# Weight and z preparation cut into stages a step apart, in an attention and GLU kernel

## Chip, core, metric

One of the eight cores of a Trainium2 chip runs the whole kernel. The metric is the device time of one execution in microseconds; lower is better. The time before is 2075.76 us, the median of three runs (2073.78 to 2076.12).

## What is computed

```python
scores = z @ z.T / S                      # per batch; B, S = 4, 3008; d_qk = 64
attn = np.maximum(scores, 0) ** 2
x = u * (attn @ v)                        # d_model = 256
x = x.reshape(B * S, 256)
gate = 1 / (1 + np.exp(-(x @ w_gate)))    # weights 256 x 1536, float64 in memory
out = (gate * (x @ w_val)) @ w_out        # 1536 x 256; out 12032 x 256, float32
```

The inputs u, v and z are float32. The three weights come as float64, and the kernel turns each into two 32-bit parts itself.

## The kernel before

To keep float32 accuracy every factor is split in a high part, which TensorE multiplies exactly, and a low part, the rest. A product takes three matmuls: high by high, high by low, low by high. Names that end in h or P are high parts, names in l or Q low ones.

The work is cut in *chunks* of 512 queries (448 in the last of a batch), six in each of four batches, and a chunk into 12 *steps*, one for each 256 keys. `steps` and `chunks` list them; g counts steps through the whole kernel and C counts chunks from 0. In the text "first chunk" is C = 0, steps 0 to 11, "third chunk" is C = 2, steps 24 to 35. A step has up to four pieces on TensorE (PE):

- `pe_scores` (lines 303 and 304), 4 matmuls for the step that comes next (two steps ahead while C < 2). By symmetry scores of an earlier chunk are kept: `turn` (line 343) transposes them on DVE and copies them to DRAM, and `load_back` fetches them, so that many later steps have no scores.
- `pe_pv` (lines 373 to 378), 12 matmuls: attention weights ah, al by vh, vl, summed in acc over the chunk.
- `pe_out` (lines 451 to 453), 6 matmuls into oacc, for the gated tile of two steps ago.
- `pe_gv` (lines 407 to 409), 12 matmuls: gate and value of 128 hidden units, for the chunk two before (so from C = 2 on), into gv, of which there is one buffer.

Beside them `post_scores` makes r by Relu and Square on ScalarE (ACT; lines 314, 315), then ah on ACT or DVE (323, 325) and al on VectorE (DVE; 326). `gate` takes a Sigmoid on ACT (419) and the product g on DVE (420); `split_h` makes hh on ACT and hl on DVE, `split_x` xh and xl the same way (all in lines 121 and 122). At a chunk's end `make_x` multiplies acc by the transposed u (line 384, DVE), which frees acc.

Each engine works through its instructions in program order. That order is written by hand in the main loop (lines 556 to 618), under `tc.manual_schedule()`; the calls of a step append to all engines. DMAs are issued from the SP queue, in order too. Tiles with the same tag share buffers, so a tag also sets waits.

Weights are prepared while the first chunks run, in 15 jobs (`w_jobs`): `gv` jobs for gate and value, `wo` jobs for the output weights; a *piece* is 128 by 512 words, and the first three jobs have two pieces. `load_w` fetches raw words at steps set in `w_load`. The generator `narrow_w` then makes 32-bit values from the two words of a float64: absolute value of the high word on ACT (line 159), clamp and shift (160, 161), sign (167), power of two (173), low word (175), sum (180) on DVE, the high part on ACT (181, woh or wgh), the low part on DVE (183, wol or wgl). `weights(g)` runs it up to the next `yield`: one unit a step for steps 9 to 23, ahead of `post_scores`; three units, a whole single job, at the end of each step of the third chunk. There the high part and the sum before it lie in one unit:

```python
        nc.vector.tensor_tensor(fa, fa, fb, op=ALU.add)
        nc.scalar.activation(hi, fa, AF.Copy)
        yield
```

z is loaded, transposed on DVE (`turn_z`, line 205) and split (`prep_z`: high part zP on ACT, line 215, low part zQ on DVE, line 219, and two copies to the other 64 partitions by DMA, lines 221 and 222), all in one go at every other step of the first chunk; for later batches during the chunk before, where v's low part runs on GpSimd (POOL, line 249).

Of the kernel before, what the change touches and what calls it, by code (L numbers as in the profile page):

```python
# [8 lines left out]
F32 = mybir.dt.float32  # L9
# [19 lines left out]
def kernel(  # L29
# [116 lines left out]
    def narrow_w(kind, f, raws, early):  # L146

        m = len(raws)
        if kind == "gv":
            tiles = (w_tile(f"g{x}{f // 2}")[:, f % 2 : f % 2 + m] for x in "hl")  # L150
            hi, lo = (t.rearrange("p f i k e -> p (f i k e)") for t in tiles)
        else:
            tiles = (w_tile(f"o{x}{f // 4}")[:, f % 4 : f % 4 + 2 * m] for x in "hl")
            hi, lo = (t.rearrange("p f d -> p (f d)") for t in tiles)
        part = [slice(r * CH, (r + 1) * CH) for r in range(m)]
        a = one.tile([P, m * CH], I32, tag="xh" if early else "zraw", name="wa")
        fa = a.bitcast(F32)
        for r, t in zip(part, raws):
            nc.scalar.activation(fa[:, r], t[:, :, 1].bitcast(F32), AF.Abs)
        nc.vector.tensor_scalar(fa, fa, MIN64, MAX64, op0=ALU.max, op1=ALU.min)  # L160
        nc.vector.tensor_scalar(
            a, a, 3, 0x3FFFFFF8, op0=ALU.logical_shift_left, op1=ALU.bitwise_and
        )
        if early:
            yield
        for r, t in zip(part, raws):
            nc.vector.scalar_tensor_tensor(
                a[:, r], t[:, :, 1], -0x40000000, a[:, r], op0=ALU.bitwise_and, op1=ALU.bitwise_or
            )
        yield  # L170
        b = (one if early else two).tile([P, m * CH], I32, tag="xl" if early else "vraw", name="wb")
        fb = b.bitcast(F32)
        nc.vector.tensor_scalar(b, a, -0x00800000, None, op0=ALU.bitwise_and)
        for r, t in zip(part, raws):
            nc.vector.scalar_tensor_tensor(
                fb[:, r], t[:, :, 0].bitcast(U32), 2.0**-52, fb[:, r], op0=ALU.mult, op1=ALU.mult
            )
        if early:
            yield
        nc.vector.tensor_tensor(fa, fa, fb, op=ALU.add)  # L180
        nc.scalar.activation(hi, fa, AF.Copy)  # L181
        yield
        nc.vector.tensor_tensor(lo, fa, f32(hi), op=ALU.subtract)
        yield
# [23 lines left out]
    def prep_z(b, s):  # L208
        zt = zt_t.pop((b, s))
        zP = zp.tile([P, CH], F32R, tag="zP", name="zP")  # L210
        zQ = zp.tile([P, CH], F32R, tag="zQ", name="zQ")
        if (b, s) == (0, 1):
            nc.vector.tensor_copy(zP[0:64], zt[0:64])
        else:
            nc.scalar.activation(zP[0:64], zt[0:64], AF.Copy)
        if (b, s) == (0, 0):
# [6 lines left out]
        z_t[b, s] = zP, zQ  # L223
# [231 lines left out]
    def finish(b, c, h, osb):  # L455
# [21 lines left out]
        ("gv", 4, "gh4"),  # L477
        ("gv", 5, "gl4"),
        ("wo", 4, "oh2"),
        ("gv", 6, "ol2"),  # L480
        ("gv", 7, "gh5"),
        ("wo", 6, "gl5"),
        ("gv", 8, None),
        ("gv", 9, None),
# [5 lines left out]
    w_units = [i for i in range(len(w_jobs)) for _ in range(5 if i < 3 else 3)]  # L490
    w_from = 9
    w_load = {5: [0], 7: [1], 9: [2], 12: [3], 14: [4], 17: [5], 19: [6], 24: [7], 25: [8], 28: [9], 29: [10]}
    w_load.update({30: [11], 31: [12], 32: [13], 33: [14]})
    w_raw, w_run = {}, {}

    def weights(g):

        for _ in range(0 if g < w_from else 1 if g < 2 * NPAIR else 3):
            if w_units:
                i = w_units.pop(0)  # L500
                if i not in w_run:
                    kind, f = w_jobs[i][:2]
                    w_run[i] = narrow_w(kind, f, w_raw.pop(i), i < 3)
                next(w_run[i])

    def weight_loads(g):
        for i in w_load.get(g, ()):
            kind, f, *places = w_jobs[i]
            step = 1 if kind == "gv" else 2
            w_raw[i] = [  # L510
                load_w(kind, f + n * step, place) for n, place in enumerate(places)
            ]

    with tc.manual_schedule():
# [17 lines left out]
        prep_z(0, 0)  # L532
        load_v(0, 1)
# [15 lines left out]
        prep_v_high(0, 2)  # L549
        load_v(0, 4)  # L550
        turn_z(0, 2)
        prep_z(0, 2)


        m1 = m2 = None
        for g, (b, c, k) in enumerate(steps):
            C = b * NCH + c
            ahead = g + (1 if C > 1 else 2)
            nxt = steps[ahead] if ahead < len(steps) and g != 2 * NPAIR - 1 else None
            if g < 2:  # L560
                pe_pv(b, c, k)
            if nxt:
                pe_scores(*nxt)
            if m1:
                gate(*m1)
            if k == 0 and C > 1:
                split_x(*chunks[C - 2])
            if C == 0:
                if k + 2 < NPAIR:
                    prep_v_low(0, k + 2)  # L570
                if k + 5 < NPAIR:
                    load_v(0, k + 5)
                if k % 2 == 0 and k // 2 + 4 < NCH:
                    load_z(0, k // 2 + 4)
                if k % 2 == 1 and k // 2 + 3 < NCH:
                    turn_z(0, k // 2 + 3)
                    prep_z(0, k // 2 + 3)
            if C < 2:
                weights(g)
            if nxt:  # L580
                post_scores(*nxt)
            if C == 0 and k + 3 < NPAIR:
                prep_v_high(0, k + 3)
            if g + 2 < len(steps) and back(*steps[g + 2]):
                load_back(*steps[g + 2])
            if m1:
                split_h(*m1)
            if nxt:
                turn(*nxt)
            if g >= 2:  # L590
                pe_pv(b, c, k)
            if k == (6, 4, 0)[C] if C < 3 else k == 6:
                load_u(b, c)
            if k == (10, 8, 2)[C] if C < 3 else k == 8:
                prep_u(b, c)
            if k == NPAIR - 1:
                make_x(b, c)
# [34 lines left out]
        split_x(*chunks[-2])  # L632
# [49 lines left out]
```

## Time and profile before

| | |
|---|---|
| median of three runs | 2075.76 us |
| the profiled execution: time, span | 2077.04 us, 2075.3 us |
| busy: PE, DVE, ACT, POOL | 97%, 57%, 43%, 3% |
| mean granted clock of TensorE | 0.992 of full |
| chain that ended last: PE, DVE, ACT, DMA | 78%, 7%, 6%, 4% |

The profile shows one execution. The span runs from its first to its last instruction; the time holds some 1.7 us more around it. PE's busy time counts overlapping matmuls once, so its count of matmuls in a stretch says more than its busy share.

### The profile page before, as it was taken

Reading aid. Unit: us, or ns where it says so; the run is one execution under the profiler, and the core shown is the slowest. Engines: PE = TensorE matmul, PEld = TensorE weight load, DVE = VectorE, ACT = ScalarE, POOL = GpSimd, SP = SyncE. Lnnn points to the kernel's source line nnn. Section 1 sums busy time; section 2 is a strip of 40 time slices with the busy share of each in tenths; the row PEclk is TensorE's granted clock in tenths of the full one; section 3 lists DMA queues with packets and bytes.
Section 4 is the critical chain, followed back from the end, with each engine's and each line's share of the span. In section 5 each row is a group of like instructions: output and inputs, shape, how many; then the busy total and the mean of one; then the engine's idle time right before and its main releaser. Section 6 shows DMA issues by size and latency. Waiting matters only on the chain.

```text
span 2075.3 us, 24548 instructions
## 1 busy us (share of the span) xinstructions
PE 2009.8 (97%) x9356; PEld 1772.9 (85%) x9356; DVE 1182.3 (57%) x1552; ACT 901.9 (43%) x1202; POOL 55.5 (3%) x44
## 2 busy tenths in 40 slices
PE   8977799999999999999999999999999999999999
PEld 6755688898899888889889888888889988888988
DVE  6766655456666555455666564545666655545443
ACT  7745434445444434344444443434544443433332
POOL 0000000011000000002000000001200000000000
PEclk9999999999999999999999999999999999999999
DMA  5302223242535252335344352425353525233101
GB/s 135 102 31 61 49 51 69 42 114 71 93 63 113 46 118 46 95 80 143 64 87 72 77 97 53 110 50 145 76 92 64 113 47 116 46 94 70 56 11 20
DMA packets 689910, 159.86 MB, mean 77 GB/s; under 512 B 640768, under 2 KB 668416, under 8 KB 689792
## 3 DMA queue, kind: packets, MB, share of 16 engines
q1 hardware_dynamic: 688736, 158.17, 35.1%
q8 instruction: 73, 1.20, 0.2%
q14 instruction: 45, 0.37, 0.1%
q10 hardware_dynamic: 1056, 0.13, 0.0%
HBM read 88.74 MB, written 63.44 MB: 73 GB/s over the span
## 4 chain that ended last, share of the span: by engine, by line
PE 78%; DVE 7%; ACT 6%; DMA 4%; SPq 3%; issue 2%; DVEq 0%; ACTq 0%
PE gv L408 10%; PE gv L409 10%; PE gv L407 10%; PE acc L373 9%; PE acc L378 9%; PE acc L375 9%; PE oacc L453 5%; PE oacc L452 5%; PE oacc L451 5%; PE sc L304 3%; PE sc L303 3%; DMA vraw<-in_v_dram 2%; ACT r L315 1%; ACT r L314 1%; DMA r<-turned 1%
## 5 line engine op out<-in xcount | busy, mean ns | idle before, releaser
L419 ACT ACTIVATE g<-gv 128x512 f32<-128x512 f32 (+1 forms) x288 | 168.6, 586 | 864.8 <-PE gv L409 857.3
L407 PE MATMUL gv<-x,wgh 128*128 128x512 f32 (+1 forms) x1152 | 437.3, 380 | 36.4 <-DVE g L420 34.4
L420 DVE TENSOR_TENSOR g<-gv,g 128x512 f32<-128x512 f32 (+1 forms) x288 | 195.2, 678 | 478.3 <-ACT g L419 478.3
L373 PE MATMUL acc<-ah,vh 128*128 128x512 f32 (+1 forms) x1152 | 429.8, 377 | 11.0 <-DVE ut L384 5.3
L408 PE MATMUL gv<-x,wgh 128*128 128x512 f32 (+1 forms) x1152 | 436.3, 379 | 2.2 <-DVE x L122 2.2
L409 PE MATMUL gv<-x,wgl 128*128 128x512 f32 (+1 forms) x1152 | 435.6, 378 | 0.0
L375 PE MATMUL acc<-ah,vl 128*128 128x512 f32 (+1 forms) x1056 | 396.9, 376 | 0.4 <-DVE vl L249 0.4
L326 DVE TENSOR_TENSOR al<-r,ah 128x1024 fp32r<-128x1024 f32 (+1 forms) x288 | 346.4, 1203 | 76.8 <-ACT ah L323 68.1
L378 PE MATMUL acc<-al,vh 128*128 128x512 f32 (+1 forms) x1152 | 339.5, 376 | 3.2 <-DVE al L326 2.7
L407 PEld LDWEIGHTS gv<-x,wgh 128*128 128x128 f32 x1152 | 219.8, 191 | 69.2 <-DVE g L420 40.1
L373 PEld LDWEIGHTS acc<-ah,vh 128*128 128x128 f32 x1152 | 218.3, 189 | 42.2 <-DVE ut L384 6.0
L325 DVE CAST ah<-r 128x1024 fp32r<-128x1024 f32 (+1 forms) x164 | 113.0, 689 | 244.1 <-ACT r L315 244.0
L378 PEld LDWEIGHTS acc<-al,vh 128*128 128x128 f32 x1152 | 217.8, 190 | 32.7 <-DVE al L326 7.1
L408 PEld LDWEIGHTS gv<-x,wgh 128*128 128x128 f32 x1152 | 220.0, 191 | 29.4 <-DVE x L122 3.2
L409 PEld LDWEIGHTS gv<-x,wgl 128*128 128x128 f32 x1152 | 220.3, 191 | 26.7
L375 PEld LDWEIGHTS acc<-ah,vl 128*128 128x128 f32 x1056 | 200.2, 190 | 25.1 <-DVE vl L249 0.8
L451 PE MATMUL oacc<-hh,woh 128*128 128x512 f32 (+1 forms) x576 | 215.9, 375 | 1.3 <-ACT woh L181 1.3
L453 PE MATMUL oacc<-hh,wol 128*128 128x512 f32 (+1 forms) x576 | 215.9, 375 | 0.0
L452 PE MATMUL oacc<-hl,woh 128*128 128x512 f32 (+1 forms) x576 | 215.8, 375 | 0.0
L122 DVE TENSOR_TENSOR hl<-g,hh 128x512 fp32r<-128x512 f32 (+1 forms) x288 | 201.7, 700 | 18.2 <-ACT hh L121 18.2
L314 ACT ACTIVATE r<-sc 128x1024 f32<-128x1024 f32 (+1 forms) x186 | 188.5, 1014 | 37.0 <-PE sc L304 36.5
L315 ACT ACTIVATE r<-r 128x1024 f32<-128x1024 f32 (+1 forms) x186 | 195.5, 1051 | 5.9
(51 smaller groups left out, 1611.5 us busy)
## 6 DMA issues: line engine op xcount, KB each, us to landing
turned<-turned SPq DMA_DIRECT2D x780, 64.0 KB, 1.9
r<-turned SPq DMA_DIRECT2D x66, 512.0 KB, 4.0
r<-turned SPq DMA_DIRECT2D x36, 448.0 KB, 4.1
vraw<-in_v_dram SPq DMA_DIRECT2D x44, 256.0 KB, 3.1
uraw<-in_u_dram SPq DMA_DIRECT2D x160, 64.0 KB, 2.5
out_dram<-osb SPq DMA_DIRECT2D x160, 64.0 KB, 1.9
wraw<-in_moe_w_gate_dram SPq DMA_DIRECT2D x12, 256.0 KB, 3.8
wraw<-in_moe_w_val_dram SPq DMA_DIRECT2D x12, 256.0 KB, 4.2
```

Of the source, the lines that this page charges most:

```text
L314: nc.scalar.activation(by_halves(r[:, :, 0:n]), products(sc[:, :, 0:n]), AF.Relu, scale=scale)
L315: nc.scalar.activation(r[:, :, 0:n], r[:, :, 0:n], AF.Square)
L326: nc.vector.tensor_tensor(al[:, :, 0:n], r[:, :, 0:n], f32(ah[:, :, 0:n]), op=ALU.subtract)
L373: nc.tensor.matmul(o, vh[:, j, ds], moving(ah[:, j, 0:n]), start=(k == 0 and j == 0), stop=False)
L375: nc.tensor.matmul(o, vl[:, j, ds], moving(ah[:, j, 0:n]), start=False, stop=False)
L378: nc.tensor.matmul(acc[:, d, 0:n], vh[:, j, ds], moving(al[:, j, 0:n]), start=False, stop=last)
L407: nc.tensor.matmul(o, wh, moving(xh[:, d, 0:n]), start=(d == 0), stop=False)
L408: nc.tensor.matmul(o, wh, moving(xl[:, d, 0:n]), start=False, stop=False)
L409: nc.tensor.matmul(o, wl, moving(xh[:, d, 0:n]), start=False, stop=(d == NB - 1))
L451: nc.tensor.matmul(o, wh, moving(hh[:, 0:n]), start=(f == 0), stop=False)
L452: nc.tensor.matmul(o, wh, moving(hl[:, 0:n]), start=False, stop=False)
L453: nc.tensor.matmul(o, wl, moving(hh[:, 0:n]), start=False, stop=(f == NF - 1))
```

## The change

- `narrow_w` becomes a class `Narrow` with one method for each stage. `plan` places the stages of a job at fixed steps: ACT's Abs at the end of step `start`, shift, sign, power, low words and sum in the steps behind, the high part on ACT at the head of a step after the sum's, the low part at that step's end. `w_before` runs ahead of `post_scores`, `w_after` behind `split_h`.
- There are ten jobs: eight of two pieces and two of one. Jobs 0 to 3 run in five stages, 4 to 7 in three (`low_by_piece` does power, low words and sum of one piece after the other), 8 and 9 in one. Loads, raw tiles and scratch tiles move accordingly; the transposed-copy tag `vraw` serves as scratch for jobs 8 and 9 alone.
- In the first chunk z's transpose, high part and low part stand at different places: transpose at even steps, high part at the end of the next step, low part with its two copies the step after that. At the start z's third piece is loaded ahead of v's second and transposed before the first `post_scores`.
- At a chunk's last step `pe_pv` stands ahead of `gate`, and, from C = 2 on, `make_x` directly behind `gate`, ahead of the next `post_scores`. u is loaded and transposed at other steps in the first three chunks.
- `split_x` of the last chunk but one stands at the end of the last step, ahead of the last `gate`.

```diff
+    w_jobs = [
+        ("gv", 0, "oh1", "ol1"),
...
+    def plan(i, start):
+        def at(when, g, *ops):
+            when.setdefault(g, []).extend((i, op) for op in ops)
+        at(w_after, start, ("abs",))
+        if i < 4:
+            at(w_before, start + 1, ("shift",), ("sign", 0))
+            at(w_before, start + 2, ("sign", 1), ("power",))
+            at(w_before, start + 3, ("low_words",))
+            at(w_before, start + 4, ("add",))
+            at(w_before, start + 5, ("high_part",))
+            at(w_after, start + 5, ("low_part",))
+        elif i < 8:
+            at(w_before, start + 1, ("shift",), ("sign", 0), ("sign", 1))
+            at(w_before, start + 2, ("low_by_piece",))
+            at(w_before, start + 3, ("high_part",))
+            at(w_after, start + 3, ("low_part",))
+        else:
+            at(w_before, start + 1, ("shift",), ("sign", 0), ("low_by_piece",))
+            at(w_after, start + 1, ("high_part",), ("low_part",))
+
+    for i, start in enumerate([6, 10, 14, 18, 23, 25, 27, 29, 32, 33]):
+        plan(i, start)
...
+            end = k == NPAIR - 1
             if g < 2:
                 pe_pv(b, c, k)
             if nxt:
                 pe_scores(*nxt)
+            if end:
+                pe_pv(b, c, k)
             if m1:
                 gate(*m1)
+            if end and C > 1:
+                make_x(b, c)
             if k == 0 and C > 1:
                 split_x(*chunks[C - 2])
...
+                if k % 2 == 0 and 3 <= k // 2 + 2 < NCH:
+                    prep_z_low(0, k // 2 + 2)
+                if k % 2 == 0 and k // 2 + 3 < NCH:
+                    turn_z(0, k // 2 + 3)
                 if k % 2 == 0 and k // 2 + 4 < NCH:
                     load_z(0, k // 2 + 4)
-                if k % 2 == 1 and k // 2 + 3 < NCH:
-                    turn_z(0, k // 2 + 3)
-                    prep_z(0, k // 2 + 3)
-            if C < 2:
-                weights(g)
+            weights(w_before.get(g, ()))
             if nxt:
                 post_scores(*nxt)
             if C == 0 and k + 3 < NPAIR:
                 prep_v_high(0, k + 3)
+            if C == 0 and k % 2 == 1 and k // 2 + 3 < NCH:
+                prep_z_high(0, k // 2 + 3)
...
             if m1:
                 split_h(*m1)
+            weights(w_after.get(g, ()))
             if nxt:
                 turn(*nxt)
-            if g >= 2:
+            if g >= 2 and not end:
                 pe_pv(b, c, k)
+            if end and C < 2:
+                make_x(b, c)
...
-            if k == NPAIR - 1:
-                make_x(b, c)
...
                 pe_gv(*m1)
-                weights(g)
...
+            if g == len(steps) - 1:
+                split_x(*chunks[-2])
...
         gate(*m1)
-        split_x(*chunks[-2])
         split_h(*m1)
```

How this moves instructions, from the listed order of both programs. First DVE around the end of the first weight job, at the turn from the first to the second chunk. Before (wa and wb are the job's two scratch tiles, wgl its low part; the high part on ACT stands between lines 180 and 325 in the program):

```order
L326 TENSOR_TENSOR al<-r,ah 128x1024 [waits PE_49,Activation_49]
L384 TENSOR_TENSOR ut<-acc,ut 128x1024 [waits PE_49]
L180 TENSOR_TENSOR wa<-wa,wb 128x1024 [waits DVE_49]
L325 CAST ah<-r 128x1024 [waits Activation_49]
L326 TENSOR_TENSOR al<-r,ah 128x1024 [waits DVE_49]
L183 TENSOR_TENSOR wgl<-wa,wgh 128x1024
```

Now (the scratch tiles are named wo and wx after their tags; line 188 is the sum, 211 the low part, 359 and 360 are ah and al, 165 to 172 the next job):

```order
L359 CAST ah<-r 128x1024 [waits PE_49,Activation_49]
L360 TENSOR_TENSOR al<-r,ah 128x1024 [waits DVE_49,PE_49]
L188 TENSOR_TENSOR wo<-wo 128x1024
L359 CAST ah<-r 128x1024 [waits PE_49,Activation_49]
L360 TENSOR_TENSOR al<-r,ah 128x1024 [waits DVE_49,PE_49]
L315 STREAM_TRANSPOSE ut<-uraw 128x512 [waits DMAHW4_49,DMAHW6_49,DMAHW2_49,DMAHW0_49]
L315 STREAM_TRANSPOSE ut<-uraw 128x512 [waits DMAHW5_49,DMAHW7_49,DMAHW3_49,DMAHW1_49]
L165 TENSOR_SCALAR wx<-wx 128x1024 [waits Activation_49]
L166 TENSOR_SCALAR wx<-wx 128x1024 [waits DVE_49]
L172 SCALAR_TENSOR_TENSOR wx<-wraw,wx 128x512 [waits DVE_49]
L360 TENSOR_TENSOR al<-r,ah 128x1024 [waits PE_49,Activation_49]
L211 TENSOR_TENSOR wgl<-wo,wgh 128x1024
```

Between the sum and the low part there was one pair of ah and al, with the high part ahead of that pair on ACT; now two steps' work lies between them.

Next DVE in the third chunk. Before, a whole single job stood in one row:

```order
L420 TENSOR_TENSOR g<-gv,g 128x512 [waits Activation_49]
L326 TENSOR_TENSOR al<-r,ah 128x1024 [waits Activation_49]
L122 TENSOR_TENSOR hl<-g,hh 128x512 [waits Activation_49]
L160 TENSOR_SCALAR wa<-wa 128x512 [waits Activation_49]
L161 TENSOR_SCALAR wa<-wa 128x512 [waits DVE_49]
L167 SCALAR_TENSOR_TENSOR wa<-wraw,wa 128x512 [waits DVE_49]
L173 TENSOR_SCALAR wb<-wa 128x512 [waits DVE_49]
L175 SCALAR_TENSOR_TENSOR wb<-wraw,wb 128x512 [waits DVE_49]
L180 TENSOR_TENSOR wa<-wa,wb 128x512 [waits DVE_49]
L183 TENSOR_TENSOR wgl<-wa,wgh 128x512 [waits Activation_49]
```

Now (lines 454, 360 and 122 are g, al and hl; wz is the scratch of one piece):

```order
L454 TENSOR_TENSOR g<-gv,g 128x512 [waits Activation_49]
L165 TENSOR_SCALAR wo<-wo 128x1024
L166 TENSOR_SCALAR wo<-wo 128x1024 [waits DVE_49]
L172 SCALAR_TENSOR_TENSOR wo<-wraw,wo 128x512 [waits DMAHW2_49,DVE_49]
L172 SCALAR_TENSOR_TENSOR wo<-wraw,wo 128x512 [waits DMAHW3_49]
L360 TENSOR_TENSOR al<-r,ah 128x1024 [waits Activation_49]
L122 TENSOR_TENSOR hl<-g,hh 128x512 [waits Activation_49]
L211 TENSOR_TENSOR wgl<-wo,wgh 128x1024
L454 TENSOR_TENSOR g<-gv,g 128x512 [waits Activation_49]
L194 TENSOR_SCALAR wz<-wo 128x512
L195 SCALAR_TENSOR_TENSOR wz<-wraw,wz 128x512 [waits DVE_49]
L198 TENSOR_TENSOR wo<-wo,wz 128x512 [waits DVE_49]
```

The job's shift and sign stand between g and al of one step, its low words and sums between g and al of the next, and the low part (211) of another job behind hl.

Last DVE at the end of a chunk (the fourth). Before:

```order
L420 TENSOR_TENSOR g<-gv,g 128x512 [waits Activation_49]
L325 CAST ah<-r 128x1024 [waits Activation_49]
L326 TENSOR_TENSOR al<-r,ah 128x1024 [waits DVE_49]
L122 TENSOR_TENSOR hl<-g,hh 128x512 [waits Activation_49]
L384 TENSOR_TENSOR ut<-acc,ut 128x1024 [waits PE_49]
L420 TENSOR_TENSOR g<-gv,g 128x512 [waits Activation_49]
L122 TENSOR_TENSOR x<-ut,x 128x1024 [waits Activation_49]
```

Now (line 418 is the product with u, 359 and 360 are ah and al of the next chunk's first step):

```order
L454 TENSOR_TENSOR g<-gv,g 128x512 [waits Activation_49]
L418 TENSOR_TENSOR ut<-acc,ut 128x1024 [waits PE_49]
L359 CAST ah<-r 128x1024 [waits Activation_49]
L360 TENSOR_TENSOR al<-r,ah 128x1024 [waits DVE_49]
L122 TENSOR_TENSOR hl<-g,hh 128x512 [waits Activation_49]
L454 TENSOR_TENSOR g<-gv,g 128x512 [waits Activation_49]
L122 TENSOR_TENSOR x<-ut,x 128x1024 [waits Activation_49]
```

The product with u stood behind ah, al and hl; it stands behind g and ahead of them.

## Rows read from the trace of the kernel before

**Rows 1.** Page, part 1: engine, busy us (share of the span), instructions.

```profile
PE 2009.8 (97%) x9356; PEld 1772.9 (85%) x9356; DVE 1182.3 (57%) x1552; ACT 901.9 (43%) x1202; POOL 55.5 (3%) x44
```

**Rows 2.** Busy time by stage: length, PE, PEld, DVE, ACT, POOL (x instructions), PEclk, DMA.

```profile
13.60:116.80 103.20, 89.42 (x382) 70.69 (x380) 75.79 (x91) 73.00 (x81) 0.00 (x0) 0.98 0.44 117
116.80:251.30 134.50, 99.94 (x401) 81.47 (x401) 90.58 (x137) 63.71 (x84) 0.00 (x0) 0.92 0.20 42
```

**Rows 3.** Whole run, what PE waited for: us in total, times, longest.

```profile
PE gv L407 <- DVE g L420: 34.4, 13, 4.6
PE acc L373 <- DVE ut L384: 5.3, 4, 2.1
```

**Rows 4.** Waits of DVE, then of ACT, from 13.6 to 251.3 us, same columns.

```profile
DVE al L326 <- ACT ah L323: 40.7, 18, 4.2
...
DVE wb L173 <- DMA turned<-turned: 7.6, 6, 1.3
...
ACT wgh L181 <- DVE wa L180: 56.2, 10, 6.9
ACT woh L181 <- DVE wa L180: 30.5, 5, 6.9
ACT zP L215 <- DVE zt L205: 9.0, 4, 2.8
```

**Rows 5.** DVE in time order, third chunk: start, length, instruction, idle before.

```profile
159.64 1.23 DVE L326 TENSOR_TENSOR al<-r,ah 128x1024 fp32r<-128x1024 f32 x1 [2.28 <-ACT ah L323]
...
161.39 0.42 DVE L160 TENSOR_SCALAR wa<-wa 128x512 f32<-128x512 f32 x1
...
165.93 0.69 DVE L183 TENSOR_TENSOR wgl<-wa,wgh 128x512 fp32r<-128x512 f32 x1 [0.70 <-ACT wgh L181]
166.54 0.68 DVE L420 TENSOR_TENSOR g<-gv,g 128x512 f32<-128x512 f32 x1
169.51 1.22 DVE L326 TENSOR_TENSOR al<-r,ah 128x1024 fp32r<-128x1024 f32 x1 [2.28 <-ACT ah L323]
```

**Rows 6.** DVE in time order, second chunk.

```profile
70.79 0.69 DVE L325 CAST ah<-r 128x1024 fp32r<-128x1024 f32 x1 [3.12 <-ACT r L315]
```

**Rows 7.** PE in time order, line 407 in three steps.

```profile
167.28 0.48 PE L407 MATMUL gv<-x,wgh 128*128 128x512 f32 x1 [2.26 <-DVE g L420]
...
287.74 0.38 PE L407 MATMUL gv<-x,wgh 128*128 128x512 f32 x1
...
295.08 0.38 PE L407 MATMUL gv<-x,wgh 128*128 128x512 f32 x1
```

**Rows 8.** All engines in time order, end of the first batch.

```profile
493.17 0.69 DVE L420 TENSOR_TENSOR g<-gv,g 128x512 f32<-128x512 f32 x1 [2.89 <-ACT g L419]
...
495.17 0.69 DVE L325 CAST ah<-r 128x1024 fp32r<-128x1024 f32 x1 [1.32 <-ACT r L315]
...
496.25 2.00 POOL L249 TENSOR_TENSOR vl<-vraw,vh 128x512 fp32r<-128x512 f32 x1 [2.24 <-ACT vh L241]
...
497.04 1.76 DVE L122 TENSOR_TENSOR hl<-g,hh 128x512 fp32r<-128x512 f32 x1
...
498.73 1.08 DVE L384 TENSOR_TENSOR ut<-acc,ut 128x896 f32<-128x896 f32 x1
...
499.86 0.48 PE L373 MATMUL acc<-ah,vh 128*128 128x512 f32 x1 [2.14 <-DVE ut L384]
```

**Rows 9.** PE in time order, just after the last step.

```profile
1977.52 0.48 PE L407 MATMUL gv<-x,wgh 128*128 128x512 f32 x1 [1.63 <-ACT x L121]
1978.78 0.80 PE L408 MATMUL gv<-x,wgh 128*128 128x512 f32 x1 [0.78 <-DVE x L122]
```

**Rows 10.** Busy time by window, columns of rows 2: the two places above.

```profile
500.00:510.00 10.00, 10.00 (x39) 8.48 (x40) 6.14 (x8) 6.58 (x9) 1.86 (x2) 0.83 0.21 54
...
1980.00:1990.00 10.00, 10.00 (x44) 8.55 (x43) 3.51 (x6) 1.82 (x3) 0.00 (x0) 0.90 0.02 3
```

**Rows 11.** Page, part 6: DMA issues, count, KB each, us to landing.

```profile
wraw<-in_moe_w_val_dram SPq DMA_DIRECT2D x12, 256.0 KB, 4.2
```

More of the change, by code (lines that the diff above doesn't have):

```diff
@@ L144, in load_w, with __init__, scratch, abs @@
         return t.rearrange("p k f e -> p (k f) e")
[L146 to L166, printed above, removed]
+    class Narrow:
+        def __init__(self, kind, f, raws, a_tag, b_tag):
+            self.kind, self.f, self.raws, self.m = kind, f, raws, len(raws)
+            self.a_tag, self.b_tag = a_tag, b_tag
+            self.part = [slice(r * CH, (r + 1) * CH) for r in range(self.m)]
+        def scratch(self, tag, m):
+            return (two if tag == "vraw" else one).tile([P, m * CH], I32, tag=tag, name="w" + tag[0])
+        def abs(self):
+            self.a = self.scratch(self.a_tag, self.m)
+            self.fa = self.a.bitcast(F32)
+            for r, t in zip(self.part, self.raws):
+                nc.scalar.activation(self.fa[:, r], t[:, :, 1].bitcast(F32), AF.Abs)
+        def shift(self):
+            a, fa = self.a, self.fa
+            nc.vector.tensor_scalar(fa, fa, MIN64, MAX64, op0=ALU.max, op1=ALU.min)
+            nc.vector.tensor_scalar(
+                a, a, 3, 0x3FFFFFF8, op0=ALU.logical_shift_left, op1=ALU.bitwise_and
+            )
+        def sign(self, n):
+            r, t = self.part[n], self.raws[n]
@@ L167, in narrow_w @@
             nc.vector.scalar_tensor_tensor(
-                a[:, r], t[:, :, 1], -0x40000000, a[:, r], op0=ALU.bitwise_and, op1=ALU.bitwise_or
+                self.a[:, r], t[:, :, 1], -0x40000000, self.a[:, r], op0=ALU.bitwise_and, op1=ALU.bitwise_or
             )
[L170 to L184, printed above, removed]
+        def power(self):
+            self.b = self.scratch(self.b_tag, self.m)
+            nc.vector.tensor_scalar(self.b, self.a, -0x00800000, None, op0=ALU.bitwise_and)
+        def low_words(self):
+            fb = self.b.bitcast(F32)
+            for r, t in zip(self.part, self.raws):
+                nc.vector.scalar_tensor_tensor(
+                    fb[:, r], t[:, :, 0].bitcast(U32), 2.0**-52, fb[:, r], op0=ALU.mult, op1=ALU.mult
+                )
@@ L476 @@
         ("wo", 0, "gh2", "gl2"),
[L477 to L484, printed above, removed]
+        ("gv", 4, "gh4", "gl4"),
+        ("gv", 6, None, None),
+        ("wo", 4, "gh5", "gl5"),
+        ("gv", 8, "gh4", "gl4"),
+        ("gv", 10, "gh5", "gl5"),
         ("wo", 8, None),
-        ("gv", 10, None),
-        ("gv", 11, None),
         ("wo", 10, None),
@@ L489 @@
     ]
[L490 to L504, printed above, removed]
+    w_load = {3: 0, 6: 1, 9: 2, 13: 3, 19: 4, 24: 5, 25: 6, 27: 7, 26: 8, 29: 9}
@@ L506, in weight_loads, with weights @@
+    for i, start in enumerate([6, 10, 14, 18, 23, 25, 27, 29, 32, 33]):
+        plan(i, start)
+    def weights(ops):
+        for i, (op, *which) in ops:
+            if i not in w_run:
+                w_run[i] = Narrow(*w_jobs[i][:2], w_raw.pop(i), *w_scratch[i])
+            getattr(w_run[i], op)(*which)
     def weight_loads(g):
-        for i in w_load.get(g, ()):
+        if g in w_load:
+            i = w_load[g]
             kind, f, *places = w_jobs[i]
             step = 1 if kind == "gv" else 2
-            w_raw[i] = [
-                load_w(kind, f + n * step, place) for n, place in enumerate(places)
-            ]
+            w_raw[i] = [load_w(kind, f + n * step, place) for n, place in enumerate(places)]
```

50 lines of the change are left out of this document (41 added, 9 removed).

## Prediction

> **What bounds the kernel now.** I read the page's engine shares first: TensorE (PE) is busy 97% of the span [rows 1]. That is too flattering, because matmuls overlap in the records, so I counted matmuls instead. Where nothing holds PE, line 407 starts one step at 287.74 and the next at 295.08, 7.34 us for 34 matmuls, 0.216 us each [rows 7]. The windows by stage come next. The first and second chunk, from 13.6 to 116.8 us, hold 382 matmuls, 82.5 us of work in 103.2 us. The third, up to 251.3, holds 401, 86.6 us of work in 134.5 us [rows 2]. So 20.7 + 47.9 = 68.6 us are lost there, waits and half-clock time together; mean clock in the third chunk is 0.92 [rows 2]. The rest of the run loses little.
>
> The waits name the cause. PE waits 34.4 us for the gate product of VectorE (DVE), line 420, nearly half of that loss [rows 3]. DVE is late because it and ScalarE (ACT) take turns: ACT waits 86.7 us (56.2 + 30.5) with the high part of a weight job, line 181, for DVE's sum. Since the next Relu and ah stand behind that high part in ACT's order, DVE then waits 40.7 us for ah [rows 4]. One step shows the loop: from one al (159.64) to the next (169.51) 9.87 us pass, with DVE idle 0.70 us for the high part and 2.28 us for ah; at the end of it PE has stood 2.26 us [rows 5, 7]. In the second chunk one such turn holds DVE 3.12 us [rows 6]. DVE is busy 75.8 of 103.2 and 90.6 of 134.5 us, ACT less: no engine is full, the order costs the time [rows 2].
>
> **Step 1: weights a stage a step apart.** One single piece costs DVE 5.15 us from line 160's start (161.39) to the next g (166.54); less the 0.70 us wait that is 4.45 us [rows 5]. Before, 3 doubles and 12 singles are 18 pieces; after, 8 doubles and 2 singles are 18 too. Those ending ahead of the third chunk rise from 6 pieces to 8, those in it fall from 12 to 10. I count a double as two singles and leave the saved instructions as margin.
>
> *First two chunks.* DVE: 75.8 + 2 × 4.45 = 84.7 us of work, against PE's 82.5 [rows 2, 5]. The bounds are 84.7 (all waits gone) and 103.2 (none gone). ACT's 73.0 grow by some 2 us for the extra Abs and high part and still fit. I take 90, nearer the lower end: the high part is now issued at least a step after its sum, so waits like the 3.12 us [rows 6] lose their cause; what is late next is DVE's own sum, heaviest in the last six steps of the first chunk, where low halves of v, z and the first job meet. Gain 13.
>
> *Third chunk.* DVE: 90.6 - 2 × 4.45 = 81.7 us against PE's 86.6, ACT less than its 63.7 [rows 2, 5]. PE becomes the bound. Now DVE runs shift, signs and low words of a job between g and al, just where it stood 2.28 us for ACT's ah, and the high part's 0.70 us wait goes because its sum was made a step earlier [rows 5]. The 7.6 us that line 173 waited for the turned-copy DMAs go as well, save for the two single jobs, the only ones still using that buffer [rows 4]. Ends: 86.6 and 134.5. I take 91, near the lower end, because each wait in the loop has work put over it; a step without its two waits is 9.87 - 2.98 = 6.9 us for DVE, under PE's 7.34, but the copies' transposes of the last six steps come on top, so a few us are left for DVE running late. Gain 43.5.
>
> **Step 2: z's stages apart.** ACT waits 9.0 us in 4 turns for z's transposed tile [rows 4]; the transpose now stands a step ahead and the low half with its two SP copies a step behind. This lies inside the 13 above and is not added. The copies leave SP about a step later than before, but still two steps ahead of the scores that read them. Weight loads move ahead of some v loads on SP (job 0 after step 3, not 5); each piece takes about 4.2 us to land [rows 11], and v is used two steps after its load, so I cost it at nothing; with that cover gone it would be a few us once. POOL's queue isn't touched.
>
> **Step 3: the product with u ahead of the next attention weights.** At the end of a batch the product starts at 498.73, behind the slow hl (497.04, 1.76 us), and PE stands 2.14 us; four such ends cost 5.3 us [rows 3, 8]. The clock then averages 0.83 of full in 500 to 510 us, between its levels of 1.2 and 2.4 GHz, another 1.7 us [rows 10]. Now the product stands behind g: 493.17 + 0.69 + 1.08 = 494.9, while the cast behind it can't start before 495.17, since ACT releases it then [rows 8]. So the move is free by some 0.2 us. Next late is x for the new chunk: z's transpose stays behind hl, and g, ACT's xh and DVE's xl follow, so PE, 2 us earlier, will meet xl about 1 us late once. Between 0 and 7.0 I take 4.5. The other ends, at which PE doesn't wait now, gain nothing.
>
> Here a rule bears on the step. The row: POOL's low half of v starts at 496.25, just after al (which follows the 0.69 us cast at 495.17), and hl behind takes 1.76 us, where g of the same size takes 0.69 [rows 8]. The Trainium skill, SBUF — State Buffer, section "SBUF: two separate sides", says that VectorE, with two SBUF inputs, and GpSimd lock a shared port pair for a whole instruction, and "the other fully blocks". By that rule an al that slips past 496.25 would wait for all of POOL's instruction, and the gain of this step would be near 0 instead of 4.5; this is the third rival.
>
> **Step 4: x of the last chunk but one split ahead of the last gate.** After the last step PE waits 1.63 us for xh and 0.78 for xl [rows 9], and the clock averages 0.90 in the following window, 1.0 us more [rows 10]. Its input was ready a chunk ago; in ACT's order it just stood behind a Sigmoid. Bounds 0 and 3.4; I take 3.4.
>
> **Sum.** 13 + 43.5 + 4.5 + 3.4 = 64.4 us. The profiled execution took 2077.04 us (span 2075.3), 1.3 above the median 2075.76. On the median's scale: 2075.8 - 64.4 = 2011.4, I say 2011. With every stage at its lower end, 18.5 + 47.9 + 7.0 + 3.4 = 76.8, it would be 1999.
>
> **Rivals.**
> 1. *DVE becomes the brake.* The order is better, but in the heavy steps DVE's chain still sets the pace, now by work instead of waits: al and g slip a step further each time and PE stands again before line 407. For it: in the first two chunks DVE's sum exceeds PE's, and in the third it is 94% of PE's. Against it: after a gate's matmuls PE has 22 others (4 scores, 12 attention, 6 out), 22 × 0.216 = 4.8 us, before it needs the next g. If the 12 steps of the third chunk each take the 9.87 us of the present lighter steps [rows 5], the chunk takes 118 instead of 91 and the time is about 2038.
> 2. *The raw weights land late.* Ten jobs each wait a piece's 4.2 us [rows 11]: 42 us, 2053. Against it: most jobs are loaded three steps or more ahead of use.
> 3. *The port rule at batch ends.* 2016, within the range; it needs a slip of 0.35 us or more.
> 4. *Slower.* The product with u waits for the chunk's last attention matmuls, and now the cast, al and hl of the next chunk queue behind it on DVE, at 22 chunk ends. After those matmuls PE has 18 others (6 out, 12 gate and value), 18 × 0.216 = 3.9 us, before it needs the new ah; product and cast take 1.9 us. It decides once DVE starts the product over 2 us late. If every end then cost what 499.86 shows, 2.14 + 1.7 us [rows 8, 10], that is 22 × 3.84 = 84 against 60 won elsewhere: 2100, and slower from 16 such ends on. Against it: g is the only work ahead of the product there.
> That the change doesn't do what it says is unlikely: the listed order shows each move.
>
> **How the numbers follow.** Forecast 2011: 0.66 (own range 2002 to 2020). Rival 1: 0.20, 2020 to 2045. Rival 2: 0.04. Rival 3: 0.06. Rival 4: 0.04. The range 2002 to 2038 holds the forecast, rival 3 and most of rival 1; about 0.15 stays outside. Within 0.2% (4.2 us, about what a measurement of this kernel tells from no change) is only a stray mixture, 0.01; slower 0.04; faster 0.95.
>
> **What the changed profile would show.** Step 1: waits of ACT's high parts for DVE fall from 86.7 to under 10 us, those of PE for g from 34.4 to under 5; the first gate matmul of the fourth chunk starts near 195 instead of 251 us, with the clock near 1.0 up to there. If PE still waits for g while DVE has no idle time, rival 1 holds. Step 2: waits for zt nearly gone in the first chunk. Step 3: the first attention matmul of a chunk no longer waits for the product, and there is a short one for xl at one batch end. Step 4: no wait for x after the last step. The prediction is wrong if the third chunk keeps over 105 us, or if new waits for al follow the chunk ends.

## Result and profile after

The changed kernel takes **2012.84 us**, median of 4 runs (2012.01 to 2013.97), against 2075.94 for the kernel before, run beside it on the same chip: ratio 0.9696, 95% interval 0.9679 to 0.9713. The forecast was 2011.0. The profiled execution took 2012.01 us, its span 2010.2. Ratios below are all to the kernel before, run beside the other on its chip; they come from all runs of both and can differ in the fourth digit from the quotient of the medians.

TensorE's (PE) share on the page answers to [rows 1]:

```profile
PE 1990.6 (99%) x9356; PEld 1767.4 (88%) x9356; DVE 1177.9 (59%) x1535; ACT 903.6 (45%) x1197; POOL 55.2 (3%) x44
```

Busy time by stage, as [rows 2]; the windows are cut so that they hold about the matmuls of the two windows there:

```profile
13.60:106.80 93.20, 85.90 (x381) 72.44 (x380) 81.91 (x99) 77.09 (x86) 0.00 (x0) 0.96 0.45 113
106.80:198.00 91.20, 87.81 (x398) 75.55 (x398) 80.13 (x111) 61.69 (x75) 0.00 (x0) 0.98 0.35 77
```

The first window had 103.20 us for 382 matmuls before, the second 134.50 for 401: 10.0 and 43.3 us gone, the second less 0.6 for three matmuls at 0.216. That is 53 of the 63 us; the rest is at the ends of batches, after the last step, and in no stage that was looked at. The first gate matmul of the fourth chunk starts at 198.86, where the prediction had it near 195.

What PE waited for in the whole run answers to [rows 3]; the 34.4 us for g are 1.9, and the product with u (now line 418, output ut) has gone from the list (columns: us in total, times, longest):

```profile
PE sc L337 <- DMA zP<-zQ: 5.2, 1, 5.2
PE acc L412 <- DVE al L360: 2.9, 2, 2.7
PE gv L441 <- DVE g L454: 1.9, 2, 1.1
```

One wait at the top is new: 5.2 us, once, for z's SP copies. The waits of DVE and ACT from 13 to 200 us answer to [rows 4]. ACT's waits with a high part (woh, wgh, now line 208) fall from 86.7 us to 8.1, DVE's for ah from 40.7 to 6.3, and none for zt is left:

```profile
ACT g L453 <- DVE hl L122: 18.0, 9, 4.4
...
ACT woh L208 <- DVE wz L198: 6.5, 2, 5.0
DVE al L360 <- ACT ah L357: 6.3, 7, 3.0
...
DVE wv L194 <- DMA turned<-turned: 3.4, 2, 2.8
...
ACT woh L208 <- DVE wo L188: 1.2, 1, 1.2
...
ACT wgh L208 <- DVE wx L188: 0.4, 1, 0.4
```

At the end of the first batch, in time order (start, length, instruction, idle before), the product with u runs at 439.64, straight behind g, where [rows 8] had it behind hl, and PE has no wait there:

```profile
438.78 0.69 DVE L454 TENSOR_TENSOR g<-gv,g 128x512 f32<-128x512 f32 x1 [2.83 <-ACT g L453]
439.64 1.09 DVE L418 TENSOR_TENSOR ut<-acc,ut 128x896 f32<-128x896 f32 x1 [0.17 <-PE acc L412]
...
441.51 1.23 DVE L360 TENSOR_TENSOR al<-r,ah 128x1024 fp32r<-128x1024 f32 x1
...
441.87 2.00 POOL L283 TENSOR_TENSOR vl<-vraw,vh 128x512 fp32r<-128x512 f32 x1 [2.26 <-ACT vh L275]
...
442.66 1.77 DVE L122 TENSOR_TENSOR hl<-g,hh 128x512 fp32r<-128x512 f32 x1
```

The granted clock is 1.00 around this end and from 1900 to 1940 us, past the last step ([rows 10] has both places before):

```profile
1900.00:1940.00 40.00, 40.00 (x190) 35.65 (x189) 19.07 (x27) 14.57 (x22) 0.00 (x0) 1.00 0.08 14
437.00:447.00 10.00, 10.00 (x50) 8.98 (x49) 7.26 (x8) 6.05 (x9) 3.28 (x2) 1.00 0.09 31
```

### The profile page after: what moved, and what is told of

Read it like the earlier page. It is cut to its first block, busy times and chain, and to the rows that moved or that the text cites. A ratio compares the mean times of both kernels' runs of the same rounds, so it can differ in the third digit from the quotient of the medians.

```text
span 2010.2 us, 24546 instructions
## 1 busy us (share of the span) xinstructions
PE 1990.6 (99%) x9356; PEld 1767.4 (88%) x9356; DVE 1177.9 (59%) x1535; ACT 903.6 (45%) x1197; POOL 55.2 (3%) x44
## 4 chain that ended last, share of the span: by engine, by line
PE 88%; DVE 5%; ACT 2%; DMA 2%; SPq 2%; issue 1%; DVEq 0%; ACTq 0%
PE gv L442 11%; PE gv L441 11%; PE gv L443 11%; PE acc L412 10%; PE acc L407 10%; PE acc L409 10%; PE oacc L485 6%; PE oacc L487 6%; PE oacc L486 6%; PE sc L337 3%; PE sc L338 3%; DVE al L360 1%; DMA vraw<-in_v_dram 1%; ACT r L348 1%; DVE hl L122 1%
## 5 line engine op out<-in xcount | busy, mean ns | idle before, releaser
L441 PE MATMUL gv<-x,wgh 128*128 128x512 f32 (+1 forms) x1152 | 431.9, 375 | 2.0 <-DVE g L454 1.9
L442 PE MATMUL gv<-x,wgh 128*128 128x512 f32 (+1 forms) x1152 | 431.9, 375 | 0.8 <-DVE x L122 0.7
L360 DVE TENSOR_TENSOR al<-r,ah 128x1024 fp32r<-128x1024 f32 (+1 forms) x288 | 346.0, 1201 | 34.4 <-ACT ah L357 25.7
L441 PEld LDWEIGHTS gv<-x,wgh 128*128 128x128 f32 x1152 | 217.7, 189 | 29.4 <-DVE g L454 3.5
L442 PEld LDWEIGHTS gv<-x,wgh 128*128 128x128 f32 x1152 | 217.7, 189 | 27.9 <-DVE x L122 2.2
```

What stands on the lines that cost most here:

```text
L360: nc.vector.tensor_tensor(al[:, :, 0:n], r[:, :, 0:n], f32(ah[:, :, 0:n]), op=ALU.subtract)
L441: nc.tensor.matmul(o, wh, moving(xh[:, d, 0:n]), start=(d == 0), stop=False)
L442: nc.tensor.matmul(o, wh, moving(xl[:, d, 0:n]), start=False, stop=False)
```

## Experiments

### The three small parts, each alone on the kernel before

**a_product**: the product with u moved, nothing else.

```diff
+            end = k == NPAIR - 1 and C > 1
...
+            if end:
+                pe_pv(b, c, k)
             if m1:
                 gate(*m1)
+            if end:
+                make_x(b, c)
```

> The kernel before with the chunk-end move alone (attention matmuls written ahead of the gate, the product with u ahead of the next attention weights, from the third chunk on). My theory: PE no longer waits 5.3 us for the product at four batch ends and keeps its clock at the first one; x is late once: 4.5 us faster than before, 2071.4. Rival (port pair and late x eat it): no change, 2075.9. Rival (al of the next chunk late at every end): slower, over 2080.

Measured: 2070.27 us (6 runs) against 2076.02; ratio 0.9970 [0.9959, 0.9981], 5.8 us less. At the first batch's end the product starts at 493.42 instead of 498.73, and the window of [rows 10] is at full clock:

```profile
492.81 0.69 DVE L420 TENSOR_TENSOR g<-gv,g 128x512 f32<-128x512 f32 x1 [2.88 <-ACT g L419]
493.42 1.08 DVE L384 TENSOR_TENSOR ut<-acc,ut 128x896 f32<-128x896 f32 x1
...
500.00:510.00 10.00, 9.68 (x46) 8.15 (x45) 6.51 (x9) 7.26 (x10) 1.46 (x2) 1.00 0.22 54
```

The window holds 46 matmuls where it held 39. The part works alone, and rival 4 (waits for al at 22 chunk ends) isn't there.

**a_last_x**: x of the last chunk but one split ahead of the last gate.

```diff
+            if g == len(steps) - 1:
+                split_x(*chunks[-2])
...
         gate(*m1)
-        split_x(*chunks[-2])
```

> The kernel before with the early split of x of the last chunk but one alone. My theory: the 2.4 us wait after the last step and the half-clock stretch behind it go: 3.4 us faster, 2072.5. Rival: the wait only moves to the next release, no change, 2075.9.

Measured: 2073.34 us (11 runs), ratio 0.9988 [0.9979, 0.9997]: 2.7 us less, the interval 0.6 to 4.4. PE's waits of [rows 9] are gone, and the second window of [rows 10] is at full clock, with 48 matmuls instead of 44:

```profile
1980.00:1990.00 10.00, 10.00 (x48) 8.75 (x47) 5.85 (x9) 3.48 (x6) 0.00 (x0) 1.00 0.22 38
```

**a_z**: z's stages and the order of the start, with the weights as before.

```diff
+                if k % 2 == 0 and 3 <= k // 2 + 2 < NCH:
+                    prep_z_low(0, k // 2 + 2)
...
-                if k % 2 == 1 and k // 2 + 3 < NCH:
-                    turn_z(0, k // 2 + 3)
-                    prep_z(0, k // 2 + 3)
...
+            if C == 0 and k % 2 == 1 and k // 2 + 3 < NCH:
+                prep_z_high(0, k // 2 + 3)
```

> The kernel before with z's stages and the start alone, weights as before. My theory: ACT's 9 us of waits for the transpose go, but only the first eight steps were held by them: 2 to 5 us faster, 2072. Rival: the later copies of z to the other partitions meet the loads of v and weights and PE waits for them, as it does for 5.2 us in the changed kernel: no change or slower, 2075 to 2079.

Measured: 2071.75 us (12 runs), ratio 0.9980 [0.9971, 0.9988]: 4.3 us less. ACT's 9.0 us for zt are gone, but PE has a wait of 2.20 us at 42.87 for a z copy that the kernel before doesn't have. If the three parts add, they make 12.8 us, and some 50 are left for the weights.

### The gap between a sum and its high part

**b_high_same_step**: the changed kernel with the high part of jobs 0 to 7 back in the step of its sum. Doubles, loads and the rest stay.

```diff
-            at(w_before, start + 4, ("add",))
-            at(w_before, start + 5, ("high_part",))
-            at(w_after, start + 5, ("low_part",))
+            at(w_before, start + 4, ("add",), ("high_part",))
+            at(w_after, start + 4, ("low_part",))
...
-            at(w_before, start + 2, ("low_by_piece",))
-            at(w_before, start + 3, ("high_part",))
-            at(w_after, start + 3, ("low_part",))
+            at(w_before, start + 2, ("low_by_piece",), ("high_part",))
+            at(w_after, start + 2, ("low_part",))
```

> The changed kernel with the high part of jobs 0 to 7 put back into the step of its sum, ahead of the next Relu on ACT; pieces, loads and all else stay. My theory (the stage gap takes the wait away): each of eight jobs again holds ACT for DVE and then DVE for ah by 2 to 4 us, 16 to 30 us slower than 2012.8, so 2029 to 2043. Rival (fewer, larger instructions and the earlier two pieces make the gain): within 4 us of 2012.8.

Measured: 2040.24 us, ratio 0.9827 [0.9813, 0.9842]: 27.4 us slower than the changed kernel. The waits of 13 to 230 us show the loop of [rows 4] back, on DVE and on ACT:

```profile
DVE al L360 <- ACT ah L357: 24.8, 10, 4.2
...
ACT wgh L208 <- DVE wo L198: 15.6, 3, 5.3
```

So one step between sum and high part is worth 27 of the weights' 50 us. The windows with about the same matmuls say where: the first two chunks take 104.8 us, 11.6 more than in the changed kernel and 1.6 more than before, the third 105.2, 14.0 more than in the changed kernel but some 28 less than before:

```profile
13.60:118.40 104.80, 89.12 (x381) 71.23 (x380) 81.67 (x98) 75.33 (x86) 0.00 (x0) 0.98 0.39 103
118.40:223.60 105.20, 93.92 (x397) 76.93 (x398) 80.49 (x112) 61.74 (x76) 0.00 (x0) 0.95 0.30 64
```

PE now loses its time to r and to ah, not to g (13 to 230 us):

```profile
PE sc L337 <- ACT r L348: 9.5, 7, 2.2
PE acc L407 <- ACT ah L357: 4.9, 5, 1.0
...
PE gv L441 <- DVE g L454: 0.2, 1, 0.2
```

Of the 34.4 us that PE waited for g before, 32.5 lay in the third chunk, and they don't come back (the kernel before, 116.8 to 251.3 us):

```profile
PE gv L407 <- DVE g L420: 32.5, 11, 4.6
```

So the other 28 us won there don't come from the gap between sum and high part. What stays in this run is the rest of the change: before, a job's whole row stood ahead of g, 5.15 us of DVE [rows 5]; now all of its stages but the low part stand behind g, and there are doubles, earlier loads and another spread over the chunks. That the place behind g is what takes the wait for g away is likely from the order, but no run changes it alone.

### The copies of z behind the weight loads

In the changed kernel SP issues, in time order, the four loads of job 0 (line 134, 256 KB each) just ahead of z's copies, and PE then stands:

```profile
27.27 2.00 SPq L134 DMA_DIRECT2D wraw<-in_moe_w_gate_dram  x1
...
30.34 0.47 SPq L134 DMA_DIRECT2D wraw<-in_moe_w_val_dram  x1
...
31.42 0.47 SPq L252 DMA_DIRECT2D zQ<-zP  x1
31.98 0.54 SPq L253 DMA_DIRECT2D zP<-zQ  x1
...
38.73 0.77 PE L337 MATMUL sc<-zP 128*128 128x512 f32 x1 [5.18 <-DMA zP<-zQ]
```

The two copies, issued at 31.42 and 31.98, take 6.4 and 6.6 us to land (KB each, us to landing):

```profile
zQ<-zP SPq DMA_DIRECT2D x1, 128.0 KB, 6.4
zP<-zQ SPq DMA_DIRECT2D x1, 128.0 KB, 6.6
```

Before, copies issued at 31.12 and 31.84 took 2.2 us each, with the weight loads only from 40.82 on. PE's stand also costs clock; the window that holds it, and the next:

```profile
30.00:40.00 10.00, 4.82 (x20) 3.89 (x19) 6.17 (x9) 5.18 (x7) 0.00 (x0) 0.80 0.97 242
40.00:50.00 10.00, 10.00 (x41) 8.48 (x41) 6.76 (x9) 7.92 (x10) 0.00 (x0) 0.86 0.91 179
```

**c_load0_later** moves the loads away:

```diff
-    w_load = {3: 0, 6: 1, 9: 2, 13: 3, 19: 4, 24: 5, 25: 6, 27: 7, 26: 8, 29: 9}
+    w_load = {5: 0, 6: 1, 9: 2, 13: 3, 19: 4, 24: 5, 25: 6, 27: 7, 26: 8, 29: 9}
...
-    for i, start in enumerate([6, 10, 14, 18, 23, 25, 27, 29, 32, 33]):
+    for i, start in enumerate([7, 10, 14, 18, 23, 25, 27, 29, 32, 33]):
```

> The changed kernel with job 0's raw loads behind step 5 instead of step 3 and the whole of job 0 one step later. Theory: the longest wait left on TensorE, 5.18 us at 38.73 for z's two SP copies (issued 31.42 and 31.98, landed 38.6), comes from job 0's four 256 KB loads (issued 27.27 to 30.8) and v's loads, with which the copies share the DMA engines; the clock of 0.60 in 35:40 and 0.72 in 40:45 behind it costs some 3 us more. With the loads away from there the wait falls under 1 us and the time to 2005 +- 2 us, 8 under the changed kernel. Rival: the copies are late because they leave SP about a step later than before; then the wait stays over 4 us and the time within 2 us of 2012.8. Second rival: the loads only meet the next copies instead; the wait moves by two steps and keeps its size.

Measured: 2010.56 us against 2076.91, ratio 0.9679 [0.9666, 0.9692]. The forecast of 2005 was missed. The interval overlaps the changed kernel's, so by times alone no gain is shown. The second rival held in part: the loads (32.09 to 33.65) now stand ahead of the next copies, and the wait is found there, smaller:

```profile
35.93 0.53 SPq L252 DMA_DIRECT2D zQ<-zP  x1
36.88 0.48 SPq L253 DMA_DIRECT2D zP<-zQ  x1
...
42.59 0.45 PE L337 MATMUL sc<-zP 128*128 128x512 f32 x1 [1.95 <-DMA zP<-zQ]
```

**e_copies_first** leaves the loads and moves the copies ahead of them:

```diff
-                if k % 2 == 0 and 3 <= k // 2 + 2 < NCH:
-                    prep_z_low(0, k // 2 + 2)
...
             weights(w_after.get(g, ()))
+            if C == 0 and k % 2 == 1 and k // 2 + 3 < NCH:
+                prep_z_low(0, k // 2 + 3)
```

> The changed kernel with z's low half and its two SP copies for pieces 3 to 5 at the end of the step that makes the high half, ahead of that step's weight loads, instead of in the next step behind them; job 0's loads stay where the change put them. Theory (the copies are late because they stand behind four 256 KB loads): with the copies ahead of the loads the 5.18 us wait of TensorE falls under 1 us and the time to 2005 to 2009 us. Rival (the DMA engines are simply full between 27 and 45 us, whatever the order): the copies or the v loads behind stay late, a wait of 2 us or more remains there, and the time is above 2010. Price of the edit if VectorE then waits for ScalarE's high half: up to 3 times 1 us, in the first chunk.

Measured: 2009.05 us against 2076.24, ratio 0.9673 [0.9660, 0.9687]. This interval, too, overlaps the changed kernel's; the trace shows the gain. The copies go out at 28.64 and 30.25, ahead of the loads, and land in 2.2 us. PE's wait for them is gone (one of 0.66 us for the next copies is left, at 40.69), and the first two chunks do 402 matmuls at full clock in the time of 381:

```profile
28.64 0.47 SPq L252 DMA_DIRECT2D zQ<-zP  x1
30.25 0.47 SPq L253 DMA_DIRECT2D zP<-zQ  x1
30.77 0.58 SPq L134 DMA_DIRECT2D wraw<-in_moe_w_gate_dram  x1
```

```profile
zQ<-zP SPq DMA_DIRECT2D x1, 128.0 KB, 2.2
zP<-zQ SPq DMA_DIRECT2D x1, 128.0 KB, 2.2
```

```profile
13.60:106.80 93.20, 88.94 (x402) 74.76 (x401) 87.28 (x105) 81.12 (x90) 0.00 (x0) 1.00 0.44 115
```

21 matmuls at 0.216 are 4.5 us. The DMA engines are still busy (share 0.84 from 30 to 40 us), and the next two copies, issued at 35.29 and 36.10 behind the loads, take 4.8 and 4.4 us. So it is the place behind the loads on SP's queue that makes a copy late; whether the copy stands in line there or shares the engines with the loads, these runs don't separate. The Trainium skill, DMA: Bandwidth & Descriptors, section "Two DMAs through the same engine are not ordered", says that within one queue of one DMA engine descriptors start in order; the copies' 6.4 and 6.6 us behind four loads and 2.2 ahead of them agree.

### The single jobs' wait for the turned copies

DVE stands 2.82 us ahead of a single job's scratch tile, and PE then misses al (changed kernel, third chunk):

```profile
176.82 0.43 DVE L194 TENSOR_SCALAR wv<-wz 128x512 int32<-128x512 int32 x1 [2.82 <-DMA turned<-turned]
...
179.89 1.22 PE L412 MATMUL acc<-al,vh 128*128 128x512 f32 x2 [2.69 <-DVE al L360]
```

**c_in_place** writes jobs 8 and 9 over their own raw words:

```diff
-                b = self.scratch(self.b_tag, 1)
+                b = self.scratch(self.b_tag, 1) if self.b_tag else t[:, :, 1]
...
-    w_scratch += [("oh2", "zraw"), ("ol2", "zraw")] * 2 + [("zraw", "vraw")] * 2
+    w_scratch += [("oh2", "zraw"), ("ol2", "zraw")] * 2 + [("zraw", None)] * 2
```

> The changed kernel with jobs 8 and 9, the two single ones, writing the power and low words over the raw tile's own high words instead of into the tile that the turned copies pass through. Theory: VectorE's 2.82 us at 176.82 behind the copies' DMAs is what makes al late and gives TensorE's 2.69 us wait at 179.89; the wait goes and, with what the clock loses behind it, the time falls by 2.5 to 5 us, to 2008 to 2010. Rival: the next turned copy or the next g is late in its place (VectorE is busy 80.1 of the third chunk's 91.2 us), and the time stays within 1.5 us of 2012.8.

Measured: 2011.57 us, ratio 0.9685 [0.9672, 0.9698]. That interval overlaps the changed kernel's, so by times alone the gain isn't shown; the trace shows the wait gone, with 409 matmuls in the third chunk's window where there were 398 (2.4 us):

```profile
106.80:198.00 91.20, 89.65 (x409) 76.97 (x410) 82.69 (x114) 62.27 (x76) 0.00 (x0) 1.00 0.34 74
```

### Together

**c_both** is c_load0_later and c_in_place; **e_copies_in_place** is e_copies_first and c_in_place; **e_copies_both** is all three edits.

> Both edits together, job 0 later and jobs 8 and 9 in place. They are 140 us apart and share no tile, so if both theories hold the gains add: 2001 to 2003 us, with TensorE waiting under 4 us in all before 200 us. If one of them fails, the time is that of the other alone.

> The same copies ahead of the weight loads, with jobs 8 and 9 in place as in the run before, which was 2.3 us under the changed kernel. If the gains add: 2003 to 2007 us.

> All three edits: copies ahead of the weight loads, job 0 one step later, jobs 8 and 9 in place. The run with the last two left TensorE one wait of 2.6 us for a z copy behind job 0's loads; with the copies ahead of them it goes too: 2003 to 2006 us. If the loads' later place costs instead (job 0 late for its Abs), it is no better than the run without it.

Measured: c_both 2008.38 us (0.9668 [0.9655, 0.9681]), where 2001 to 2003 was hoped for; a wait of 2.6 us for a z copy stays. e_copies_in_place 2007.31 (0.9667 [0.9654, 0.9680]), e_copies_both 2008.19 (0.9670 [0.9657, 0.9683]). The best, e_copies_in_place, is 5.5 us under the changed kernel; its slowest run (2008.97) is under the changed kernel's fastest, though the two ratio intervals just touch. Once the copies go first, moving job 0 shows no further gain.

### Is PE or DVE the bound of the third chunk?

**d_hl_twice** writes hl a second time in each of the third chunk's 12 steps:

```diff
         split(hh[:, 0:n], hl[:, 0:n], g[:, 0:n])
+        if again:
+            nc.vector.tensor_tensor(hl[:, 0:n], g[:, 0:n], f32(hh[:, 0:n]), op=ALU.subtract)
...
-                split_h(*m1)
+                split_h(*m1, again=C == 2)
```

> The changed kernel with hl, the low half of h, written twice in each of the third chunk's 12 steps: 12 more VectorE instructions of 0.68 us, 8.2 us, on its 80.1 of 91.2 us there; nothing is left out. Theory (TensorE is the bound of the third chunk, VectorE has room): VectorE rises to 88 us, most of it into its idle time, and the kernel is 0 to 3 us slower. Rival 1 of the prediction (VectorE sets the pace by its work): the third chunk grows by all of the 8.2 us and the kernel is 7 us or more slower, with TensorE waiting for g or al again.

Measured: 2021.54 us, ratio 0.9735 [0.9722, 0.9749], 7.8 us above the changed kernel's 2013.8 on this chip (0.9696 of 2076.91): nearly all of the 8.2 us. My expectation failed. But ACT's Sigmoid waits for hl (18.0 us above), so it could be that loop and not the work.

**d_al_behind_hl** adds as much at a place where the Sigmoid doesn't wait for it:

```diff
                 split_h(*m1)
+            if C == 2:
+                (ah, al), r, n = a_t[nxt], r_t[nxt], chunk(nxt[1])
+                nc.vector.tensor_tensor(al[:, 0, 0:n], r[:, 0, 0:n], f32(ah[:, 0, 0:n]), op=ALU.subtract)
```

> The changed kernel with half of al (128x512) written a second time behind hl in each of the third chunk's 12 steps: again 12 VectorE instructions of some 0.69 us, 8.2 us, but ScalarE's Sigmoid doesn't wait for these as it does for hl. Nothing is left out. If the loop hl, Sigmoid, g made hl written twice cost 7.8 us, this one falls into the 0.7 us gaps ahead of g and costs 0 to 4 us. If VectorE's work itself sets the third chunk's pace (rival 1), it costs 6 to 8.3 us too.

Measured: 2019.95 us, ratio 0.9726 [0.9712, 0.9739]: 6.8 us above 0.9696 of its 2076.24 (its interval just touches the changed kernel's; that of d_hl_twice stands clear of it). The third chunk's window, of d_hl_twice and then of this run, holds 369 and 375 matmuls instead of 398:

```profile
106.80:198.00 91.20, 83.88 (x369) 69.54 (x367) 81.09 (x115) 57.43 (x70) 0.00 (x0) 0.98 0.33 74
```

```profile
106.80:198.00 91.20, 82.37 (x375) 69.86 (x374) 83.23 (x118) 60.28 (x72) 0.00 (x0) 1.00 0.35 79
```

In d_hl_twice PE waits for g again, 6.0 us in 7 waits over the whole run (1.9 in 2 in the changed kernel); in this run it waits for al, which the added instruction (line 646) now ends:

```profile
PE acc L412 <- DVE al L646: 8.1, 6, 3.2
```

So the two add their work to different chains, to g's and to al's, and each pays for most of it: 29 and 23 matmuls less in the window are 6.3 and 5.0 us. DVE's idle time there falls from 11.1 us (91.2 less 80.1) only to 10.1 and 8.0. It is hardly a reserve; these are its waits in the changed kernel, from 106.8 to 198 us, each at a place in its order where the next instruction waits for ACT or a DMA:

```profile
DVE al L360 <- ACT ah L357: 3.8, 3, 3.0
DVE wv L194 <- DMA turned<-turned: 3.4, 2, 2.8
DVE g L454 <- ACT g L453: 2.2, 3, 0.7
```

This shows that DVE has no room for 8 us more at either place. It doesn't show that DVE sets the pace of the changed kernel. There PE waits only 3.4 us in the third chunk:

```profile
PE acc L412 <- DVE al L360: 2.7, 1, 2.7
PE gv L442 <- DVE x L122: 0.7, 1, 0.7
```

Its 398 matmuls are 86.0 of the 91.2 us, so PE is the bound but for some 5 us, with DVE not far behind. Both additions also stand in a chain that ends at PE; work on DVE that nothing waits for was not added, nor was a chunk with less work on DVE tried.

## Why the prediction was right, and where it wasn't

**What bounds.** The loop in which ACT's high part waits for DVE's sum, and DVE's al for ah, cost time as read from [rows 4, 5]: the staging removed these waits, and b_high_same_step brought them back, with 27 us. But the prediction laid PE's 34.4 us for g to the same loop, and in that run they stay away (0.2 us up to 230 us). So the loop is shown for about half of the weights' gain; the rest has another cause in the change, most likely that a job no longer stands ahead of g, which is not shown.

**First two chunks, 90 forecast, 93.2 measured.** The work on DVE was priced well (81.9 of 84.7 us). The 3 us over are the copies: with them first, 402 matmuls fit, so 382 take 93.2 - 20 × 0.216 = 88.9 us.

**Third chunk, 91 forecast, 91.2 measured** (91.8 with the three missing matmuls). DVE's 80.1 us are near the 81.7 forecast. The size was right, and PE became the bound as I said, but for some 5 us. What the reason lacked is how close DVE stands: I took its smaller sum for room, and the two d runs show none for 8 us, since the waits left in its order fill the chunk nearly to the end. Rival 1, with 118 us, did not come, but DVE is close behind. Waits left over in an order belong to an engine's price; I left them out for DVE, and the near hit of 91 hides it.

**Step 2, the step that failed.** "The copies leave SP about a step later than before, but still two steps ahead of the scores that read them" and, of the weight loads, "I cost it at nothing": the mis-sized term. The program order was two steps, but the copy that PE waited for went out at 31.98 and was wanted at 33.55, 38.73 less the 5.18 of waiting, so 1.6 us of cover against 6.6 to land. In time it left hardly later than before (31.84); what changed is its landing, 2.2 us then. It cost 4.5 us by the matmuls won back, and the prediction's "a few us once" was for v, not for z. I had looked at who reads what is loaded, and not at who else stands in SP's queue behind it.

**Step 3, 4.5 forecast, 5.8 alone** (interval 3.9 to 8.5). Free, as worked out, and nothing slipped; of the 1 us for xl that I took off, only some 0.2 is there: the weight load at 448.44 waits 0.39 for xl, and the matmul behind it starts 0.2 us late. Rival 3, the port rule: al starts at 441.51, POOL's low half of v (2.00 us) at 441.87, and hl behind takes 1.77 us instead of 0.68. The rule of the Trainium skill (SBUF — State Buffer, "SBUF: two separate sides") agrees with hl's length; al was 0.36 us ahead and escaped it (1.23 us).

**Step 4, 3.4 forecast, 2.7 alone.** PE has no wait after the last step.

**Sum.** 10.0 + 42.7 + 5.8 + 2.7 = 61.2 of the 63.1 us; the other 1.9 are in no stage that was looked at and lie within the interval of the ratio, some 3.5 us either way. That the total came so near, 64.4 against 63.1, is in part luck: term by term the forecast is 3.2 too high (the first two chunks 3 us, the third 0.8 and step 4 0.7, less the product with u, 1.3 too low), and the 1.9 us that no term holds made up for it. Rivals 2 and 4 left no trace: no wait for raw weights, and none for al at chunk ends.

## What to carry to other kernels

Where two engines take turns on one job, put a step between the half-products, so that neither has to wait in its own order: that was worth 27 us here, with the same instructions. When loads are moved ahead, price every small transfer that then stands behind them on the same queue by the time at which it is wanted, not by steps. Before you count an engine's idle time as a reserve, add to its work the waits that its order keeps; a doubled instruction shows in one run whether there is room at that place. And when an ablation brings back a loss, check that the same waits come back with it: here about half of the time came back, and the wait that had been named first did not.

## What was not expected of the hardware

A 128 KB copy within SBUF took 6.4 to 6.6 us behind four loads of 256 KB on the same queue and 2.2 us ahead of the same loads. PE stood 5.18 us up to 38.73; the granted clock is 0.80 on average from 30 to 40 us and 0.86 from 40 to 50, so it was at the lower of its levels of 1.2 and 2.4 GHz for part of both, though PE was busy in all of the second. The two windows hold 61 matmuls, with the copies ahead of the loads 91 at a clock of 1.00: 30 × 0.216 = 6.5 us, 1.3 more than the stand itself. At the end of the second chunk 21 matmuls (4.5 us) of this lead are left.
